# Running the 512-token feed-forward units as pairs of 64-row matmuls on two PSUM banks

## The chip, the cores and the metric

The kernel runs on one core of a Trainium2 chip. The metric is the device time of one execution in microseconds (us). The engines are named as in the profile: PE (TensorE matmul), PEld (its weight loads), DVE (VectorE), ACT (ScalarE), POOL (GpSimd), SP (SyncE, which only issues DMAs and waits).

## The reference

A gated linear-attention recurrence feeds two gated feed-forward layers; only the layers matter here (1536 tokens, width 320, hidden width 1536).

```python
def reference(**kwargs):
    attn_out = _attn_ref(**attn_kwargs)
    x = attn_out.transpose(0, 2, 1, 3).reshape(B * S, H * D)          # 1536 x 320
    x = _moe_ref(x=x, **moe_kwargs)
    return _moe2_ref(x=x, **moe2_kwargs)

def _moe_ref(x, w_gate, w_val, w_out):
    gate = 1.0 / (1.0 + np.exp(-(x @ w_gate)))
    val = x @ w_val
    return (gate * val @ w_out).astype(np.float32)
# _moe2_ref: the same without the sigmoid
```

## The kernel before

The hidden width is cut into 12 chunks of 128, so the two layers have 24 weight chunks. The tokens are cut into blocks of 512. Precision comes from splitting: every operand is held as a rounded part ("hi") and a remainder ("lo") in fp32r, and a product is hi·hi + lo·hi + hi·lo.

The work is a list of *units*: one chunk for one block of tokens. Units 0 to 23 have 256 tokens and run among the steps of the recurrence; units 24 to 83, 60 of them, have 512 tokens and fill the rest of the program. Four units that follow each other share one block and add into the same four accumulators; such a run of four is a *segment* (segment 8 is units 24 to 27, the last is segment 22). Each unit `u` is made of named tasks, and each task is a few instructions of one engine:

- `ma`, `mb` (PE): the gate and the value product, `mm1`, eight matmuls of 512 columns each into the banks `pa` and `pb`. The contraction of 320 is two full blocks of 128 rows, three matmuls each (hi·hi, hi·lo, lo·hi), and a block `c` of 64 rows, in which the weights' hi rows and lo rows lie in the two halves of the 128 rows, so that two matmuls do it.
- `ga_` (ACT, L549): the sigmoid (a copy in layer 2) of `pa`. `gm` (DVE, L554): times `pb`. `gh_` (ACT, L560) and `gl_` (DVE, L565): hi and lo of the result.
- `mm` (PE): 12 matmuls of 320 columns into the four accumulators `acc0` to `acc3`, three each.
- `ev` (DVE, L639, or L637 and ACT L635 in a layer's first segments): the four accumulators of a segment are added into `x2tok`.
- `yt`, `yh`, `yl`: after layer 1 each of 12 token tiles is transposed on PE (L483, three matmuls), and split on ACT (L492) and DVE (L496).

Each weight chunk is prepared by tasks of its own: `w` (a DMA of 960 KB, issued by SP), `na` (ACT, L214 and L215), `nb` (DVE, L221), `ns` (DVE, L226), `nc` (DVE, L232), `nd` (L238, on DVE or POOL), `s1` (ACT, L248 to L250), `s2` (L254, DVE or POOL) and `s3` (L258 and L259, DVE or POOL). Two buffers hold the staged weights, so `w` of a chunk waits until `s2` and `s3` of the chunk two before are done.

The order of everything is written out by hand in the string `PLAN`: each engine executes its instructions in the order in which the tasks stand there, and `:V` or `:G` says whether a task runs on DVE or POOL. PSUM is eight banks in four pairs of slots (`acc`, `mm1`, `e`, `y`), and a task that takes a slot waits until the last reader of that slot's former tile is done. `pa` comes from `mm1`, `pb` and the transposes from `e`.

`ga_` waits for `ma` alone, `gm` for `ga_` and `mb`, `mm` for `gl_` of its unit, and `ma` of unit u until `ga_` of unit u-2 has read its `pa`. What such a task looks like:

```python
        task("mm" + n, "P", lambda u=u: unit_mm2(u), ["gl_" + n] + prev("mm"), use)
```

Of the kernel before, what the change touches and what calls it, by code (L numbers as in the profile page):

```python
# [95 lines left out]
ev8.0 ga_30 s39:V ma31 w11 gm29 gh_29 gl_29 ma32 ev8.3 ga_31 na10 mb30 mb31 gm30 nb10 ev8.2 ma33 ns10 nc10
mm28 nd10:G mm29 gh_30 na11 gl_30 gm31 mm30 gh_31 ga_32 gl_31 mb32 s110 mm31 s210:G mb33 s310:G ev9.5 ev9.7
gm32 w12 ev9.4 gh_32 ma34 ga_33 gm33 gl_32 mb34 ev9.6 ga_34 nb11 gh_33 ns11 ma35 nc11 nd11:V mm32 s111 ma36
s211:V s311:G mb35 gl_33 ga_35 w13 mm33 gm35 gh_35 na12 gl_35 ma37 gm34 gh_34 mb36 gl_34 ga_36 mb37 ga_37 gm36
mm34 gm37 ma38 mm35 ma39 gh_36 ev10.11 gh_37 gl_36 ev10.9 ga_38 mb39 ev10.8 gl_37 ev10.10 ga_39 nb12 mb38 ns12  # L100
# [5 lines left out]
nc15 ma48 ev12.5 nd15:V gm47 s115 yt4 ma49 ev12.7 yh4 s215:G mm44 s315:G mm45 gh_46 gl_46 yl4 mb49 gh_47 ga_48
gl_47 ga_49 mm46 gm49 mm47 gh_49 gl_49 s214:V yt7 mb48 yh7 w16 yl7 w17 yt5 ma50 gm48 ev13.10 gh_48 ev13.8
gl_48 ma51 ev13.11 ev13.9 na16 mm48 yt6 yh5 mm49 ga_50 yl5 yh6 nb16 ga_51 ns16 mb50 yl6 yt9 ma52 gm50 yh9
gh_50 yl9 gl_50 yt10 mb51 yh10 mm50 gm51 nc16 gh_51 ga_52 ma53 gl_51 nd16:G yl10 mm51 mb52 ev14.2:A ev14.1:V
na17 ma54 ga_53 nb17 ev14.3:A ns17 s116 mb53 gm52 gh_52 s316:G gl_52 yt8 ma55 ev14.0:V yh8 gm53 ga_54 yl8  # L110
# [5 lines left out]
gm61 gh_61 mb63 ga_62 gl_61 ev16.9:V ga_63 mb62 s120 na21 ma64 s220:G gm62 gm63 mm60 s320:G w22 mm61 gh_63
gl_63 nb21 ma65 gh_62 ns21 gl_62 ga_64 mb64 ga_65 mm62 gm64 mm63 mb65 gh_64 ev17.0 nc21 ma66 nd21:V gm65 na22
ev17.3 mb66 ev17.1 ev17.2 gl_64 nb22 ga_66 ma67 gh_65 ns22 nc22 mb67 gl_65 ga_67 mm64 gm67 ma68 gh_67 s121
gl_67 nd22:V mm65 gm66 s221:V ma69 gh_66 s321:V gl_66 w23 ga_68 mb69 ga_69 mm66 gm69 mm67 ma70 mb68 ma71 gm68
ev18.7 gh_68 gl_68 mb70 ga_70 na23 mb71 gm70 ev18.4 s122 ev18.5 ev18.6 ma72 nb23 gh_69 ns23 s222:G mm68 nc23  # L120
# [823 lines left out]
```

## Time and profile before

| | us |
|---|---|
| median of 2 runs (453.55 and 454.4) | 453.98 |
| the profiled execution | 453.83 |
| its span, first to last instruction | 452.0 |
| start of unit 24's first matmul | 133.46 |

All durations are read from the one profiled execution, whose own time is 1.83 us above its span and 0.15 us under the median. The granted TensorE clock is 1.00, the level of 2.4 GHz, in every stretch until the very end. A matmul's record is longer than the step from one matmul to the next, because matmuls are pipelined: what counts on PE is the step.

### The profile page before, as it was taken

What the parts mean: (1) busy time and instruction counts of PE and PEld (TensorE: products, weight loads), DVE (VectorE), ACT (ScalarE), POOL (GpSimd) and SP (SyncE); (2) the same over time, 40 slices, a digit from 0 to 9 for tenths busy, and PEclk for the clock granted to TensorE, in tenths of its full rate; (3) what the DMA queues carried; (4) which work ended last, traced back from release to release, by engine and by line L of the source; (5) the groups of instructions that cost most, each with busy time, mean ns of one, the idle gap of its engine ahead of it and who ended that gap; (6) DMA issues with size and microseconds to landing.
All of it is one profiled execution on the core that took longest, in us unless ns stands there. A gap on an engine that the chain in (4) does not pass through costs nothing.

```text
span 452.0 us, 8740 instructions
## 1 busy us (share of the span) xinstructions
PE 441.0 (98%) x3530; PEld 394.8 (87%) x3530; DVE 298.7 (66%) x495; ACT 260.0 (58%) x455; POOL 121.6 (27%) x125
## 2 busy tenths in 40 slices
PE   8899999999999999999999999999999999999995
PEld 3577999899998989999999999897989898999995
DVE  6989999898853475747676666477574746534243
ACT  6989998787767556351656453756364425422220
POOL 3556573455143222210401320214222002300000
PEclk9999999999999999999999999999999999999998
DMA  7988534803201040220012040023122020000222
GB/s 237 261 277 286 157 113 143 293 2 119 88 0 56 33 146 30 89 87 1 9 80 87 1 175 1 0 88 96 80 88 88 0 88 1 0 1 5 55 58 59
DMA packets 10456, 39.33 MB, mean 87 GB/s; under 512 B 1840, under 2 KB 3760, under 8 KB 10416
## 3 DMA queue, kind: packets, MB, share of 16 engines
q1 hardware_dynamic: 10128, 38.45, 26.1%
q8 instruction: 28, 0.46, 0.4%
q10 hardware_dynamic: 288, 0.33, 0.2%
q14 instruction: 12, 0.10, 0.1%
HBM read 36.71 MB, written 1.97 MB: 86 GB/s over the span
## 4 chain that ended last, share of the span: by engine, by line
PE 82%; ACT 7%; DMA 4%; SPq 2%; issue 1%; DVE 1%; POOL 1%; POOLq 0%; ACTq 0%
PE pa L524 29%; PE pb L524 21%; PE acc L531 8%; PE acc L533 8%; PE acc L532 8%; PE o L441 2%; PE sp L412 2%; DMA og<-in_ogate_dram 2%; ACT cva L214 1%; DMA wst<-in_w_dram 1%; SPq L360 1%; PE st L431 1%; DMA cs<-in_cst_dram 1%; PE first L170 1%; ACT wst L215 1%
## 5 line engine op out<-in xcount | busy, mean ns | idle before, releaser
L524 PE MATMUL pa<-xb,W 128*128 128x512 f32 (+1 forms) x864 | 161.7, 335 | 1.1 <-ACT g L549 1.1
L524 PEld LDWEIGHTS pa<-xb,W 128*128 128x128 f32 x864 | 134.9, 190 | 13.8 <-ACT g L549 1.9
L524 PE MATMUL pb<-xb,W 128*128 128x512 f32 x480 | 112.6, 380 | 0.6 <-DVE g L554 0.6
L524 PEld LDWEIGHTS pb<-xb,W 128*128 128x128 f32 x480 | 89.3, 189 | 12.5 <-DVE g L554 1.0
L560 ACT ACTIVATE gh<-g 128x512 fp32r<-128x512 f32 (+1 forms) x84 | 47.5, 568 | 87.7 <-DVE g L554 44.2
L531 PE MATMUL acc<-W,gh 128*128 128x320 f32 x288 | 87.0, 302 | 0.0
L533 PE MATMUL acc<-W,gl 128*128 128x320 f32 x288 | 86.4, 300 | 0.0
L532 PE MATMUL acc<-W,gh 128*128 128x320 f32 x288 | 86.1, 299 | 0.0
L565 DVE TENSOR_TENSOR gl<-g,gh 128x512 fp32r<-128x512 f32 (+1 forms) x67 | 48.8, 735 | 44.3 <-ACT gh L560 44.0
L554 DVE TENSOR_TENSOR g<-g,pb 128x512 f32<-128x512 f32 x60 | 40.8, 685 | 55.4 <-PE pb L524 43.3
L549 ACT ACTIVATE g<-pa 128x512 f32<-128x512 f32 x60 | 35.7, 598 | 37.2 <-DVE gl L565 32.8
L531 PEld LDWEIGHTS acc<-W,gh 128*128 128x128 f32 x288 | 54.5, 189 | 1.4
L532 PEld LDWEIGHTS acc<-W,gh 128*128 128x128 f32 x288 | 54.5, 189 | 1.3
L533 PEld LDWEIGHTS acc<-W,gl 128*128 128x128 f32 x288 | 54.4, 189 | 0.4 <-DVE gl L565 0.3
L238 POOL TENSOR_TENSOR wst<-cva,wst 128x960 int32<-128x960 int32 x10 | 23.6, 2357 | 77.2 <-DVE cva L232 51.5
L214 ACT ACTIVATE cva<-wst 128x960 f32<-128x960 f32 x24 | 32.1, 1338 | 16.5 <-DVE wst L238 9.6
L254 POOL TENSOR_TENSOR W<-wst,W 128x832 fp32r<-128x832 f32 x9 | 19.2, 2137 | 71.2 <-ACT W L248 62.7
L248 ACT ACTIVATE W<-wst 128x832 fp32r<-128x832 f32 x24 | 28.6, 1191 | 13.6 <-DVE wst L238 9.9
L639 DVE SCALAR_TENSOR_TENSOR x2tok<-acc,x2tok 128x320 f32<-128x320 f32 x52 | 23.5, 484 | 15.0 <-PE acc L533 14.9
L215 ACT ACTIVATE wst<-wst 128x960 int32<-128x960 uint32 x24 | 31.1, 1295 | 0.0
L232 DVE SCALAR_TENSOR_TENSOR cva<-wst,cva 128x960 int32<-128x960 int32 x24 | 30.2, 1259 | 0.4
L565 POOL TENSOR_TENSOR gl<-g,gh 128x256 fp32r<-128x256 f32 x17 | 13.9, 818 | 35.7 <-ACT gh L560 25.8
(88 smaller groups left out, 494.2 us busy)
## 6 DMA issues: line engine op xcount, KB each, us to landing
wst<-in_w_dram SPq DMA_DIRECT2D x24, 960.0 KB
kq<-in_kqT_dram SPq DMA_DIRECT2D x12, 512.0 KB
Y<-in_kv_dram SPq DMA_DIRECT2D x24, 162.0 KB
out_dram<-x2tok SPq DMA_DIRECT2D x10, 160.0 KB
og<-in_ogate_dram SPq DMA_DIRECT2D x1, 960.0 KB
og<-in_ogate_dram SPq DMA_DIRECT2D x1, 640.0 KB
cs<-in_cst_dram SPq DMA_DIRECT2D x1, 469.0 KB
rhsE<-V SPq DMA_DIRECT2D x24, 2.0 KB
```

Of the source, the lines that this page charges most:

```text
L214: nc.scalar.activation(cva[0], hi.bitcast(F32), AF.Abs)
L215: nc.scalar.activation(lo, lo.bitcast(U32), AF.Copy, scale=2.0**-29)
L232: nc.vector.scalar_tensor_tensor(ai, hi, -0x40000000, ai, op0=ALU.bitwise_and, op1=ALU.bitwise_or)
L248: nc.scalar.activation(w[:, 0:NH], g[:, 0:NH], AF.Copy)
L524: nc.tensor.matmul(dst, w[:, w0 : w0 + P], x[:, h, cb].rearrange("p a b -> p b a"), start=(i == 0), stop=(i == 7))
L531: nc.tensor.matmul(a, gh[:, c], wh, start=st, stop=False)
L532: nc.tensor.matmul(a, gh[:, c], wl, start=False, stop=False)
L533: nc.tensor.matmul(a, gl[:, c], wh, start=False, stop=sp)
L549: nc.scalar.activation(t, pa, AF.Copy if l else AF.Sigmoid)
L554: nc.vector.tensor_tensor(t, t, pb, op=ALU.mult)
L560: nc.scalar.activation(gh, g, AF.Copy)
L565: eng.tensor_tensor(gl, g, gh.bitcast(F32), op=ALU.subtract)
```

## The change

In the 60 units of 512 tokens every matmul of 128 rows becomes a matmul of 64 rows, and two of them are issued as a pair: one on rows 0 to 63 of the array (LOW), one on rows 64 to 127 (UPP), on different PSUM banks. A unit's gate and value products are no longer one after the other: `ma` runs LOW rows into `pa` beside UPP rows into `pb` (8 pairs), `mb` the other way round (7 pairs). The 64-row block needs only hi·hi, hi·lo and lo·hi, so 30 half matmuls do what 16 full ones did: 15 pairs. The second product is split in the same way, `mm` with 6 pairs and a new task `mn` with 6, 12 pairs for 12 matmuls.

Where the halves exchange banks (from `ma` to `mb`, from `mm` to `mn`) the first pair must not start before the last pair has left its banks. It waits for an instruction on SP that does nothing but wait for the last two matmuls. `ga_` now waits for `mb`, as `pa` is complete only then. `pa` and `pb` are taken together at `ma`. The transposes of layer 1's output move from the slots `e` to `mm1`. `PLAN` is rewritten from unit 24 on into a regular pattern, one line of it before and after:

```diff
-gh_25 ma27 mb26 gl_25 mm24 nc8 k111:V gm26 ga_27 nd8:G mm25 w9 mb27 na9 ma28 gh_26 gl_26 ma29 gm27 gh_27 ga_28
+mb29 na10 mn27 ma30 ga_29 ev8.1 ev8.0 ev8.3 ev8.2 gm29 mm28 gh_29 gl_29 nb10 ns10 mb30 nc10 nd10:V mn28 w11
...
+    def side_by_side(runs, after=()):
+        turn = None
+        if after:
+            turn = nc.sync.nop()
+            for m in after:
+                tc.add_manual_dep(turn.ins, m.ins.name, sync)
+        for pair in zip(*runs):
+            last = [nc.tensor.matmul(o, w, x, start=st, stop=sp) for o, w, x, st, sp in pair]
+            if turn is not None:
+                for m in last:
+                    tc.add_manual_dep(m.ins, turn.ins.name, sync)
+                turn = None
+        return last
+
+    def tiles(rows, m):
+        a, al, c = m * 2 * P, NH + m * 2 * P, 2 * NH + m * P
+        own = [(c, 0, 2), (c, 1, 2)] if (rows is LOW) == (m == 0) else [(c, 0, 2)]
+        return [y for i in range(2) for y in ((a + i * P, 0, i), (a + i * P, 1, i), (al + i * P, 0, i))] + own
+
+    def mm1_half(f, l, x, dst, part, after):
+        w = W[l * NF + f]
+        runs = []
+        for rows, m in ((LOW, part), (UPP, 1 - part)):
+            t = tiles(rows, m)
+            runs.append([
+                (dst[m], w[rows, w0 : w0 + P], x[rows, h, cb].rearrange("p a b -> p b a"), part == 0 and i == 0, part == 1 and i == len(t) - 1)
+                for i, (w0, h, cb) in enumerate(t)
+            ])
+        return side_by_side(runs, after)
+
+    def mm2_half(f, l, gh, gl, accs, part, swap, st, sp, after):
+        w = W[l * NF + f]
+        wh, wl = (w[:, k + 4 * P : k + NH].rearrange("p (a b) -> p b a", a=2) for k in (0, NH))
+        runs = []
+        for rows, j0 in ((LOW, 2 * (part ^ swap)), (UPP, 2 - 2 * (part ^ swap))):
+            runs.append([
+                (accs[j], g[rows, j * P : (j + 1) * P], o[rows], st and part == 0 and k == 0, sp and part == 1 and k == 2)
+                for j in (j0, j0 + 1)
+                for k, (g, o) in enumerate(((gh, wh), (gh, wl), (gl, wh)))
+            ])
+        return side_by_side(runs, after)
...
     def ph_T2(s):
-        Tps[NSTEP + s] = transp(ps_tile("e", f"t2_{s}"), x2tok[:, s])
+        Tps[NSTEP + s] = transp(ps_tile("mm1", f"t2_{s}"), x2tok[:, s])
...
-        task("ga_" + n, "A", lambda u=u: unit_act(u), [("mb" if small else "ma") + n] + prev("ga_"), [("g", ["gl_" + n])] + ([("ge", ["gm" + n])] if pre else []))
+        task("ga_" + n, "A", lambda u=u: unit_act(u), ["mb" + n] + prev("ga_"), [("g", ["gl_" + n])] + ([("ge", ["gm" + n])] if pre else []))
...
+        if not small:
+            task("mn" + n, "P", lambda u=u: unit_mm2b(u), ["mm" + n])
```

The changed kernel's line numbers are shifted: L549 is every paired matmul, L603 is `gm`, L614 is `gl_`, L704 is `ev`, L485 the transposes, L533 to L535 the second product of the units of 256 tokens.

Three places show the new order. On PE, the first transposes of layer 1's output (`t2_0`) stand before the change between the second product of unit 41 and the first product of unit 43, all of them matmuls of the whole array:

```order
781 L532 MATMUL acc12_3_3088<-W9_2472,gh41_3031 128x320
782 L533 MATMUL acc12_3_3088<-W9_2472,gl41_3046 128x320
783 L483 MATMUL t2_0_3116<-cs_87,x2tok_88 128x128 x3
784 L524 MATMUL pb43_3120<-xb1_1155,W11_2729 128x512 x8
785 L524 MATMUL pa45_3140<-xb2_1729,W9_2472 128x512 x8
```

After the change they stand between `ma44` and `mm42`, and what stands around them are pairs of 64 rows:

```order
1569 L549 MATMUL pa44_3659<-xb2_1729,W8_2346 128x512
1570 L549 MATMUL pb44_3660<-xb2_1729,W8_2346 128x512
1573 L485 MATMUL t2_0_3680<-cs_87,x2tok_88 128x128 x3
1574 L549 MATMUL acc12_0_3536<-W10_2770,gh42_3623 128x320
1575 L549 MATMUL acc12_2_3538<-W10_2770,gh42_3623 128x320
```

There are 12 such groups, each between pairs now.

On DVE, around the evacuation of segment 9 (`acc9`; `g` and `gl` with a number are those of a unit, `cva11` and `wst11` belong to the preparation of chunk 11), the four additions stand before the change ahead of that preparation and among `gm` and `gl`:

```order
262 L554 TENSOR_TENSOR g31_2535<-g31_2535,pb31_2549 128x512
263 L565 TENSOR_TENSOR gl31_2625<-g31_2535,gh31_2621 128x512
264 L639 SCALAR_TENSOR_TENSOR x2tok_88<-acc9_1_2573,x2tok_88 128x320
265 L639 SCALAR_TENSOR_TENSOR x2tok_88<-acc9_3_2575,x2tok_88 128x320
266 L554 TENSOR_TENSOR g32_2623<-g32_2623,pb32_2627 128x512
267 L639 SCALAR_TENSOR_TENSOR x2tok_88<-acc9_0_2572,x2tok_88 128x320
270 L639 SCALAR_TENSOR_TENSOR x2tok_88<-acc9_2_2574,x2tok_88 128x320
271 L221 TENSOR_SCALAR cva11_2603<-cva11_2603 128x960
```

After the change they stand behind `gl32` and the four DVE steps of chunk 11:

```order
267 L603 TENSOR_TENSOR g32_2876<-g32_2876,pb32_2788 128x512
268 L614 TENSOR_TENSOR gl32_2893<-g32_2876,gh32_2891 128x512
269 L223 TENSOR_SCALAR cva11_2842<-cva11_2842 128x960
270 L228 TENSOR_SCALAR cva11_2842<-cva11_2842 128x960
271 L234 SCALAR_TENSOR_TENSOR cva11_2842<-wst11_2716,cva11_2842 128x960
272 L240 ISA wst11_2716<-wst11_2716,cva11_2842 128x960x2
273 L704 SCALAR_TENSOR_TENSOR x2tok_88<-acc9_1_2665,x2tok_88 128x320
274 L704 SCALAR_TENSOR_TENSOR x2tok_88<-acc9_3_2667,x2tok_88 128x320
```

The preparation of a chunk has moved ahead of an evacuation that PE needs for its next segment.

On PE, where the 512-token units begin (`acc7` is the second product of the last 256-token units), `pb25` follows `pa25` directly before the change:

```order
614 L524 MATMUL pa25_2275<-xb0_534,W5_1598 128x512 x7
615 L524 MATMUL pb25_2286<-xb0_534,W5_1598 128x512 [waits PE_49]
616 L524 MATMUL pb25_2286<-xb0_534,W5_1598 128x512 x7
617 L531 MATMUL acc7_0_2203<-W2_877,gh22_2231 128x320 [waits Activation_49]
```

After the change the two last small products stand inside unit 25, and the next pair waits for SP, where the load `w9` is ahead of its wait in `PLAN`:

```order
653 L549 MATMUL pa25_2291<-xb0_534,W5_1598 128x512
654 L549 MATMUL pb25_2292<-xb0_534,W5_1598 128x512
655 L533 MATMUL acc7_0_2203<-W2_877,gh22_2231 128x320 [waits Activation_49]
666 L535 MATMUL acc7_1_2204<-W3_940,gl23_2268 128x320 [waits Pool_49]
667 L549 MATMUL pb25_2292<-xb0_534,W5_1598 128x512 [waits SP_sequencer_49]
```

The matmul that exchanges banks has got a wait on SP, and one more change between whole-array and 64-row matmuls on either side.

## Rows read from the trace of the kernel before

**Rows 1.** The page, busy time of engines: us, share of the span, instructions.

```profile
PE 441.0 (98%) x3530; PEld 394.8 (87%) x3530; DVE 298.7 (66%) x495; ACT 260.0 (58%) x455; POOL 121.6 (27%) x125
```

**Rows 2.** Waits of PE from 133 to 447 us: total, times, longest.

```profile
PE pa L524 <- ACT g L549: 1.1, 1, 1.1
PE pb L524 <- DVE g L554: 0.6, 1, 0.6
```

**Rows 3.** Timeline of PE, full array: start us, length us, matmuls.

```profile
132.24 0.30 PE L531 MATMUL acc<-W,gh 128*128 128x320 f32 x1
132.38 0.30 PE L532 MATMUL acc<-W,gh 128*128 128x320 f32 x1
...
133.46 1.89 PE L524 MATMUL pa<-xb,W 128*128 128x512 f32 x8
135.19 1.89 PE L524 MATMUL pb<-xb,W 128*128 128x512 f32 x8
```

**Rows 4.** Timelines of PE and PEld near 60.8 us: 64-row matmuls of the recurrence.

```profile
60.78 0.65 PE L397 MATMUL sp<-kq,cs 40*64 40x512 f32 x2
60.80 0.68 PE L412 MATMUL sp<-kq 40*64 40x64 f32 x16
...
60.78 0.14 PEld L397 LDWEIGHTS sp<-kq,cs 40*64 40x64 f32 x2
60.79 0.14 PEld L412 LDWEIGHTS sp<-kq 40*64 40x64 f32 x2
```

**Rows 5.** Timeline of PE where it changes from 64-row to 128-row matmuls.

```profile
88.97 0.22 PE L412 MATMUL sp<-kq 40*64 40x64 f32 x2
89.13 0.40 PE L531 MATMUL acc<-W,gh 128*128 128x320 f32 x1
```

**Rows 6.** Groups of DVE by shape: busy us, mean ns; idle before, releaser.

```profile
L565 DVE TENSOR_TENSOR gl<-g,gh 128x512 fp32r<-128x512 f32 x60 | 45.4, 763 | 44.2 <-ACT gh L560 44.0
L554 DVE TENSOR_TENSOR g<-g,pb 128x512 f32<-128x512 f32 x60 | 40.8, 685 | 55.4 <-PE pb L524 43.3 <-ACT g L549 12.0
L232 DVE SCALAR_TENSOR_TENSOR cva<-wst,cva 128x960 int32<-128x960 int32 x24 | 30.2, 1259 | 0.4
L639 DVE SCALAR_TENSOR_TENSOR x2tok<-acc,x2tok 128x320 f32<-128x320 f32 x52 | 23.5, 484 | 15.0 <-PE acc L533 14.9
L238 DVE CUSTOM_DVE_ANT_0 wst<-wst,cva 128x1920 uint16<-128x1920 uint16 x14 | 19.1, 1363 | 0.4
L221 DVE TENSOR_SCALAR cva<-cva 128x960 f32<-128x960 f32 x24 | 15.9, 663 | 6.1 <-ACT cva L214 5.9
L226 DVE TENSOR_SCALAR cva<-cva 128x960 int32<-128x960 int32 x24 | 15.9, 661 | 0.5
```

**Rows 7.** Groups of ACT by shape, same columns.

```profile
L560 ACT ACTIVATE gh<-g 128x512 fp32r<-128x512 f32 x60 | 37.7, 631 | 81.2 <-DVE g L554 44.2 <-PE acc L532 36.8
L549 ACT ACTIVATE g<-pa 128x512 f32<-128x512 f32 x60 | 35.7, 598 | 37.2 <-DVE gl L565 32.8 <-PE pa L524 3.5 <-PE pb L524 0.8
L214 ACT ACTIVATE cva<-wst 128x960 f32<-128x960 f32 x24 | 32.1, 1338 | 16.5 <-DVE wst L238 9.6 <-POOL wst L238 4.7 <-DMA wst<-in_w_dram 2.1
L215 ACT ACTIVATE wst<-wst 128x960 int32<-128x960 uint32 x24 | 31.1, 1295 | 0.0
L248 ACT ACTIVATE W<-wst 128x832 fp32r<-128x832 f32 x24 | 28.6, 1191 | 13.6 <-DVE wst L238 9.9 <-POOL wst L238 3.6
...
L250 ACT ACTIVATE W<-wst 64x128 fp32r<-64x128 f32 x24 | 8.1, 336 | 0.5
```

**Rows 8.** Groups of POOL by shape, same columns.

```profile
L254 POOL TENSOR_TENSOR W<-wst,W 128x832 fp32r<-128x832 f32 x9 | 19.2, 2137 | 71.2 <-ACT W L248 62.7 <-issue 8.5
L565 POOL TENSOR_TENSOR gl<-g,gh 128x256 fp32r<-128x256 f32 x17 | 13.9, 818 | 35.7 <-ACT gh L560 25.8 <-DVE xt L473 6.2 <-PE acc L533 1.9
L258 POOL TENSOR_TENSOR W<-wst,W 64x128 fp32r<-64x128 f32 x16 | 11.9, 747 | 34.0 <-ACT W L249 25.5 <-issue 7.8
```

**Rows 9.** SP's waits: line and what it waited for, total us, times, longest.

```profile
SPq L207 <- DVE W L254: 137.0, 12, 29.7
```

More of the change, by code (lines that the diff above doesn't have):

```diff
@@ L96 @@
[L96 to L100, printed above, removed]
@@ L106 @@
[L106 to L110, printed above, removed]
@@ L116 @@
[L116 to L120, printed above, removed]
@@ L126 @@
-gh_81 ma83 gl_81 ga_82 ev21.5 out5 mb82 ga_83 mm80 gm82 mb83 gh_82 mm81 gm83 gl_82 mm82 gh_83 gl_83 mm83
-ev22.8 ev22.9 out9 ev22.10 ev22.11 out11
+mm20 gh_21 ga_22 gp22 gl_21:G gm22 nd7:G ga_23 na8 gh_22 gp23 k011:G gl_22:G mm21 s17 gm23 ma24 gh_23 gl_23:G
+nb8 ns8 s37:G mb24 nc8 nd8:V ma25 ga_24 gm24 mm22 mm23 gh_24 gl_24 s27:G w9 mb25 s18 ma26 ga_25 gm25 gh_25
+gl_25 s28:G s38:V ev7.11:V ev7.10:A mm24 mb26 na9 mn24 ma27 ga_26 gm26 mm25 gh_26 gl_26 nb9 ns9 k111:V mb27
+nc9 nd9:V mn25 w10 ma28 ga_27 gm27 mm26 gh_27 gl_27 mb28 s19 mn26 ma29 ga_28 gm28 mm27 gh_28 gl_28 s29:G s39:V
@@ new lines @@
+mb29 na10 mn27 ma30 ga_29 ev8.1 ev8.0 ev8.3 ev8.2 gm29 mm28 gh_29 gl_29 nb10 ns10 mb30 nc10 nd10:V mn28 w11
+ma31 ga_30 gm30 mm29 gh_30 gl_30 mb31 s110 mn29 ma32 ga_31 gm31 mm30 gh_31 gl_31 s210:G s310:V mb32 na11 mn30
+ma33 ga_32 gm32 mm31 gh_32 gl_32 nb11 ns11 mb33 nc11 nd11:V mn31 w12 ma34 ga_33 ev9.5 ev9.7 ev9.4 ev9.6 gm33
+mm32 gh_33 gl_33 mb34 s111 mn32 ma35 ga_34 gm34 mm33 gh_34 gl_34 s211:G s311:V mb35 na12 mn33 ma36 ga_35 gm35
+mm34 gh_35 gl_35 nb12 ns12 mb36 nc12 nd12:V mn34 w13 ma37 ga_36 gm36 mm35 gh_36 gl_36 mb37 s112 mn35 ma38
@@ new lines @@
+mb45 nc15 nd15:V mn43 w16 ma46 ga_45 ev12.4 ev12.6 ev12.5 ev12.7 gm45 yt2 mm44 yh2 yl2 gh_45 gl_45 mb46 s115
+mn44 ma47 ga_46 gm46 yt3 mm45 yh3 yl3 gh_46 gl_46 s215:G s315:V mb47 na16 mn45 ma48 ga_47 gm47 yt4 mm46 yh4
+yl4 gh_47 gl_47 nb16 ns16 mb48 nc16 nd16:V mn46 w17 ma49 ga_48 gm48 yt6 mm47 yh6 yl6 gh_48 gl_48 mb49 s116
+mn47 ma50 ga_49 ev13.10 ev13.8 ev13.11 ev13.9 gm49 yt5 mm48 yh5 yl5 gh_49 gl_49 s216:G s316:V mb50 na17 mn48
+ma51 ga_50 gm50 yt7 mm49 yh7 yl7 gh_50 gl_50 nb17 ns17 mb51 nc17 nd17:V mn49 w18 ma52 ga_51 gm51 yt10 mm50
@@ L128 @@
+mb77 mn75 ma78 ga_77 ev20.2 ev20.3 ev20.0 ev20.1 gm77 mm76 gh_77 gl_77 mb78 mn76 ma79 ga_78 gm78 mm77 gh_78
+gl_78 mb79 mn77 out1 out3 ma80 ga_79 gm79 mm78 gh_79 gl_79 mb80 mn78 ma81 ga_80 gm80 mm79 gh_80 gl_80 mb81
+mn79 ma82 ga_81 ev21.6 ev21.7 ev21.4 ev21.5 gm81 mm80 gh_81 gl_81 mb82 mn80 out7 ma83 ga_82 gm82 mm81 gh_82
+gl_82 mb83 mn81 out5 ga_83 gm83 mm82 gh_83 gl_83 mn82 mm83 mn83 ev22.8 ev22.9 out9 ev22.10 ev22.11 out11
 """
@@ L624, in unit_mm2, with mm2_part, unit_mm2b @@
         UT[u]["accs"] = dict(accs)
+        if ns == 4:
+            UT[u]["mm"] = mm2_part(u, 0, ())
+            return
         mm2(f, l, UT[u]["gh"], UT[u]["gl"], [accs[i] for i in range(ns)], f == fs[0], f == fs[-1])
+    def mm2_part(u, part, after):
+        k, f = UNITS[u]
+        l, fs, t = SEGS[k][0], SEGS[k][3], UT[u]
+        return mm2_half(f, l, t["gh"], t["gl"], t["accs"], part, fs.index(f) % 2, f == fs[0], f == fs[-1], after)
+    def unit_mm2b(u):
+        mm2_part(u, 1, UT[u]["mm"])
     def unit_evac(u, i, e):
@@ L751 @@
         task("xl" + n, "V", lambda s=s: ph_xl(s), ["xh" + n])
+    ends = lambda u: "mm" if SEGS[UNITS[u][0]][2] == 2 else "mn"
     staged = {k: [f"sg{i}" for i in range(len(OGS)) if OGS[i][2] == k] for k in {o[2] for o in OGS}}
@@ L797 @@
                 before = [f"yt{s}"]
-            task(f"ev{k}.{s}", on, (lambda e, u=u, i=i: unit_evac(u, i, e)) if len(on) > 1 else (lambda u=u, i=i: unit_evac(u, i, nc.vector)), ["mm" + n] + before)
+            task(f"ev{k}.{s}", on, (lambda e, u=u, i=i: unit_evac(u, i, e)) if len(on) > 1 else (lambda u=u, i=i: unit_evac(u, i, nc.vector)), [end + n] + before)
             if last and l and s % 2:
```

63 lines of the change are left out of this document (36 added, 27 removed).

## Prediction, made before the changed kernel ran

> **What bounds the kernel now.** I read the page first: PE is busy for 441.0 of 452.0 us, DVE for 66% and ACT for 58% [rows 1]. So the next view is who makes PE wait. From unit 24 on (133 to 447 us) PE waited twice, 1.1 and 0.6 us, both times for a gate that came late [rows 2]. The rest of those 314 us is matmul after matmul, so the stretch is worth what its steps add up to. The timeline gives the steps: eight matmuls of 512 columns take from 133.46 to 135.19 us, 0.216 each; two of 320 columns stand 0.136 apart (132.24 and 132.38, both rounded) [rows 3]. A unit is 16 × 0.216 + 12 × 0.136 = 5.09 us, and 60 units are 305 us. Loading weights costs nothing extra there: PEld is busy for 394.8 us under the 441.0 of PE [rows 1].
>
> **The change, part by part.** All is counted against the profiled execution, 453.83 us, which is 0.15 under the median.
>
> *The pairs.* What matters is whether a pair takes the step of one matmul. No pair of 64 rows by 128 columns is in the trace, but the recurrence has 64-row matmuls on different rows and banks. At 60.78 us two of 512 columns begin together (one piece, x2, 0.65 us long), and while they run sixteen of 64 columns go by on the other quarters of the array; four weight loads of 0.14 us lie within 0.15 us [rows 4]. Loads and products of different rows do run side by side. So I take 0.216 and 0.136 per pair. A unit has 15 + 12 pairs instead of 16 + 12 matmuls, and saves one step: 60 × 0.216 = **-13.0**. The bound on the bad side is that the two loads of a pair follow each other: a rival below. A bound on the good side: no step can be shorter than its columns, so -13.0 is all of it.
>
> The Trainium skill (TensorE: Matmul & The Clock Gate, "Measured speedup vs the span model") gives about 4 ns of issue per further tile; by it the sum would be 60 × 27 × 0.004 = 6.5 us higher, an estimate from that page. In rows 4 the second of two 512-column matmuls begins so close to the first that the timeline prints one start for both, and a late start need not add up where each half has its own rows; I leave it out of the sum.
>
> *Waits that go.* In the new order `nd` is on DVE throughout and each chunk is ready more than a unit before its use, so the two late gates should go: **-1.7** [rows 2].
>
> *Transposes among pairs.* Now 12 groups of whole-array transposes stand between 64-row pairs: 24 changes of tile size. Rows 5 show one: the last two 64-column matmuls start at 88.97, the first whole-array one at 89.13, 0.16 later where 0.06 is usual (sixteen in 0.68 minus one record of 0.22 [rows 4, 5]), and its record is 0.40 instead of 0.30, since its load lies bare. That is 0.20 per change, and I take the same the other way round: 24 × 0.20 = **+4.8**. Bounds: nothing, if a wait hides it, and twice that, if the two loads of a pair both lie bare.
>
> *Exchanges through SP.* There are 120. The last matmul of eight ends 0.16 after its last step (1.89 long, 1.73 between starts [rows 3]); a bare load is 0.10 [rows 5]; the passage through SP has no row, and I add 0.1 (at least nothing; at most some tenths): 0.4 us, where nothing covers it. Between `ma` and `mb` stand the six pairs of an earlier `mm` (0.82 us), between `mm` and `mn` an `mb` (1.51). So 117 cost nothing, and if that cover failed each would cost up to 0.4. Bare are `mb24`, `mn82` and `mn83`: **+1.2**. What is queued behind such a wait on SP are weight loads, which are early by several units, and in the other direction the wait can stand behind a weight load:
>
> *The beginning.* `w9` stands on SP ahead of the wait of `mb25`, and needs `s2` of chunk 7, on POOL. From the start of `ma24` ACT has `na8` (1.34 + 1.30) and `s1` of chunk 7 (1.19 + 2 × 0.34), then POOL the rest of unit 23 (0.82), `s3` (two, 0.75 each) and `s2` (2.14) [rows 7, 8]: 9.0 us. PE reaches `mb25` after 1.73 + 0.4 + 1.51 + 1.73 + 2 × 0.82 and two changes of tile size (0.4): 7.4. It waits about 1.5. Then `mm24` needs the last evacuation of segment 7, which stands on DVE behind `gl` of unit 25 and `s3` of chunk 8: from the end of `mb25` 0.16 + 0.60 + 0.69 + 0.63 + 0.76 + 0.48 = 3.3 without that `s3`, 4.8 with it at POOL's rate [rows 6 to 8]; PE has only `ma26`, 1.73. It is 1.6 to 3.1 late; I take 1.9, near the low end, as DVE's steps are the shorter ones. With three changes of tile size (0.6) the beginning costs **+4.0**; between 1.0 (nobody late) and 7.
>
> *Evacuations behind a weight chunk.* The pattern prepares a chunk every three units and evacuates every four, so once in 12 units DVE has `nb` to `nd` directly ahead of the evacuation. For segment 9: ACT has from `gh` of unit 30 to `ga` of unit 32 `s1` (1.86), `ga` and `gh` of unit 31 with `gm` between (0.60 + 0.69 + 0.63) and `na11` (2.63), 6.4 us, while PE goes from the end of `mb31` to that of `mb32` in 4.9; taking `gh` of unit 30 as done when `mb31` ends, gate 32 starts 1.5 late. From there 0.60 + 0.69 + 0.63 + 0.76, then `nb` to `nd` 0.66 + 0.66 + 1.26 + 1.36, then three evacuations of 0.48, since `mm32` begins on the accumulators that come free first and third: 8.1 [rows 6, 7]. DVE is there 9.6 us after `mb32`, PE already after 7.4 (`mn30`, `ma33`, `mm31`, `mb33`, `mn31`, `ma34`). Late by 2.1, of which a little is regained: 2.0. The same holds for the segments 12 and 18; at 15 ACT takes one of the four, and I count 0.5: **+6.5**. Bounds: nothing and 9. Otherwise DVE keeps up: in three units it has 3 × (0.69 + 0.63 waiting + 0.76) + 3.9 + 1.5 for `s3` + 1.5 = 13.1 us, PE 14.6.
>
> Sum: -13.0 - 1.7 + 4.8 + 1.2 + 4.0 + 6.5 = **+1.8, 455.6 us**. A measurement tells about 2% from no change, that is under 444.9 or over 463.1.
>
> **Rivals.**
>
> *DVE is not late.* If the evacuations and the beginning cost only the changes of tile size, it is 453.83 - 14.7 + 4.8 + 1.2 + 0.6 = 445.7, and some us less if a change of tile size is partly hidden. For it: DVE was idle 34% of the span [rows 1], and gates ready in advance would absorb 2 us. Against: the order leaves these chains no room by the count above.
>
> *SP as a queue.* The pivot is the wait for a weight load that is not ready: before the change SP spent 137 us in `w` waiting for `s2` alone [rows 9]. If each of the 14 loads after `w9` holds up a matmul as `w9` does, 1.5 us, the time is 455.6 + 21 = 476.6; it decides as soon as `s2` of the chunk two before ends later than the next wait. Against it: `w10` on stand one to two units behind the `s2` and `s3` that they need.
>
> *The two loads of a pair follow each other.* Then a pair cannot be shorter than two loads, 2 × 0.11 or so (a bare load is 0.10 [rows 5]): 27 × 0.22 = 5.9 instead of 4.87 per unit, +64 in all: 520. Rows 4 speak against it.
>
> *Weights cannot be loaded under a matmul of the same rows.* Each pair would show a load of 0.10: 60 × 27 × 0.10 = +162, 618 us. The Trainium skill says so (TensorE: Matmul & The Clock Gate, "The mechanism", under "What overlaps and what doesn't": only where the row group differs). The trace does not agree with it for whole-array matmuls: they share all rows, and PEld is busy 87% under a PE busy 98% [rows 1].
>
> *A pair is no pair.* If the halves run one after the other, a unit costs 30 × 0.216 + 24 × 0.136 = 9.7: +279, 735 us. Against: rows 4.
>
> **How the numbers follow.** The forecast has 0.60, its own range 450 to 461 (the bounds of the last two parts, not all at once). DVE not late 0.23, half of it under 444.9. SP as a queue 0.08, loads in turn 0.05, bare loads 0.02, no pairs 0.02. Faster by over 2%: 0.12. Slower: the upper edge of the forecast, 0.03, and the last four, 0.17: 0.20. Within 2%: 0.68. The range leaves out the lowest part of the second case and what lies above 470: 444 to 470.
>
> **What would show it right or wrong.** Right: pairs of 512 columns 0.216 apart and of 320 columns 0.136; PE idle about 2 us before `mm32`, `mm44` and `mm68`, put down to DVE; 1.5 us before `mb25`, put down to SP; 0.2 on either side of each transpose group; no idle time at the other exchanges. Wrong: pair steps above 0.22 and 0.14, idle PE at every `mb`, or no idle PE at the evacuations.

## The result, and the profile after

The changed kernel takes 459.37 us (459.29 and 459.45) against 453.98: a ratio of 1.0119, 95% interval 1.0075 to 1.0162. It is slower by 5.4 us, which is under 2%, but the interval does not reach 1; the forecast was 455.6, 1.6 us slower. The profiled execution took 459.29 us with a span of 457.5, 5.5 above the span before.

The page, the same row as in [rows 1]: PE is busy for 5.7 us less (435.3 against 441.0) in a span that is 5.5 longer:

```profile
PE 435.3 (95%) x5085; PEld 401.8 (88%) x5090; DVE 300.7 (66%) x512; ACT 258.0 (56%) x455; POOL 107.7 (24%) x108
```

So matmuls were saved and waits were added. The waits of PE from 133 to 452 us (engine and line waited for, total, times, longest) stand against the two of [rows 2]:

```profile
PE acc L549 <- DVE x2tok L704: 3.6, 3, 1.5
PE pb L549 <- SPq L545: 2.7, 1, 2.7
PE acc L549 <- DVE x2tok L702: 2.6, 2, 2.2
PE acc L535 <- POOL gl L614: 0.4, 1, 0.4
```

L704 and L702 are evacuations (`ev`), L545 is the exchange of `mb25` through SP. The gates of [rows 2] are gone from the list. Of 120 exchanges only one stands in it (a bare one leaves PE idle for 0.1 us, too little for the list).

Next, do pairs keep the step? The timeline of PE in `ma24` and at its exchange (start, length, tile, times):

```profile
134.36 0.38 PE L549 MATMUL pa<-xb,W 64*128 64x512 f32 x1
134.36 0.38 PE L549 MATMUL pb<-xb,W 64*128 64x512 f32 x1
134.58 0.38 PE L549 MATMUL pa<-xb,W 64*128 64x512 f32 x1
134.58 0.38 PE L549 MATMUL pb<-xb,W 64*128 64x512 f32 x1
...
135.23 0.95 PE L549 MATMUL pb<-xb,W 64*128 64x512 f32 x2
135.70 0.48 PE L549 MATMUL pa<-xb,W 64*128 64x512 f32 x1
136.02 0.38 PE L549 MATMUL pb<-xb,W 64*128 64x512 f32 x1
```

Both halves begin together (in the trace's records the second starts 3 to 4 ns behind the first), a pair every 0.216 us, as one matmul did in [rows 3]. `mb24` is an exchange with nothing to cover it: the step before it is 0.475 instead of 0.216, and the one behind it 0.32, since its load lies bare: 0.36 in all. At the 116 exchanges other than `mb24`, `mb25`, `mn82` and `mn83` the step is the usual one to 0.001 us.

A group of transposes between pairs, on PE:

```profile
241.48 0.38 PE L549 MATMUL pb<-xb,W 64*128 64x512 f32 x1
241.78 0.55 PE L485 MATMUL t<-cs,x2tok 128*128 128x128 f32 x3
242.26 0.54 PE L549 MATMUL acc<-W,gh 64*128 64x320 f32 x4
```

The step into the group (241.48 to 241.78) is 0.30 instead of 0.22, the group takes 0.48 (three steps of 0.11 would be 0.33), and the four matmuls behind it, two pairs, last 0.10 longer than elsewhere (0.54 against 0.43): 0.34 to 0.35 for the two changes of tile size, twelve times.

Now the beginning. The timeline of all engines from `ma25` to `mb25`:

```profile
137.49 1.74 POOL L614 TENSOR_TENSOR gl<-g,gh 128x256 fp32r<-128x256 f32 x1 [3.58 <-PE pa L549]
...
139.77 1.06 POOL L614 TENSOR_TENSOR gl<-g,gh 128x256 fp32r<-128x256 f32 x1 [0.54 <-ACT gh L609]
...
140.91 0.46 POOL L260 TENSOR_TENSOR W<-wst,W 64x128 fp32r<-64x128 f32 x1
...
141.40 0.30 PE L535 MATMUL acc<-W,gl 128*128 128x320 f32 x1
...
141.96 4.38 POOL L256 TENSOR_TENSOR W<-wst,W 128x832 fp32r<-128x832 f32 x2
...
143.98 0.33 SPq L209 DMA_DIRECT2D wst<-in_w_dram  x1
...
144.42 0.79 PE L549 MATMUL pb<-xb,W 64*128 64x512 f32 x1 [2.72 <-SPq L545]
144.42 0.79 PE L549 MATMUL pa<-xb,W 64*128 64x512 f32 x1
145.00 0.63 PE L549 MATMUL pb<-xb,W 64*128 64x512 f32 x1
...
145.43 0.63 PE L549 MATMUL pb<-xb,W 64*128 64x512 f32 x1
```

PE is done with `mm23` at 141.7 and has nothing to wait for but SP. SP stands at `w9`, `w9` waits for `s2` of chunk 7 on POOL (the first of the two in the row at 141.96), and goes out at 143.98; `mb25` begins behind it. Then something that was in no step of the forecast: the pairs are 0.43 apart. The same stretches with the granted clock (window, busy, instructions, clock, DMA share, GB/s):

```profile
133.60:141.50 7.90, 7.41 (x59) 1.00 0.01 2
141.50:144.40 2.90, 0.20 (x2) 0.90 0.00 0
144.40:147.40 3.00, 2.98 (x14) 0.52 0.78 266
```

Behind a stretch in which PE stood still for 2.7 us the clock fell to the level of 1.2 GHz for about seven pairs, some 1.4 us more. After that PE waited 2.2 us at `mm24` for `ev7.11` (L702 in the list of waits).

Last, one of the evacuations behind a chunk, `mm32`, on DVE and PE:

```profile
186.94 0.69 DVE L614 TENSOR_TENSOR gl<-g,gh 128x512 fp32r<-128x512 f32 x1 [0.75 <-ACT gh L609]
187.54 0.65 DVE L223 TENSOR_SCALAR cva<-cva 128x960 f32<-128x960 f32 x1
...
190.50 1.18 DVE L240 CUSTOM_DVE_ANT_0 wst<-wst,cva 128x1920 uint16<-128x1920 uint16 x1
191.58 0.90 DVE L704 SCALAR_TENSOR_TENSOR x2tok<-acc,x2tok 128x320 f32<-128x320 f32 x2
192.22 0.37 PE L549 MATMUL acc<-W,gh 64*128 64x320 f32 x1 [1.47 <-DVE x2tok L704]
```

`gl` of unit 32 ends at 187.6, then DVE has 4 us of chunk 11, and only then the additions, for which `mn31`, whose last matmul ends at 189.0, had been ready.

To put the whole together I took, step by step from the first pair to the last, how far apart two starts are beyond the usual step (0.216, 0.136, 0.109), in both traces:

| term | predicted | measured |
|---|---|---|
| one step of 512 columns less in 60 units | -13.0 | -13.0 |
| waits that go | -1.7 | -2.9 |
| changes of tile size at 12 transpose groups | +4.8 | +4.2 |
| bare exchanges `mb24`, `mn82`, `mn83` | +1.2 | +1.2 (0.36, 0.49, 0.36) |
| the beginning, up to `mm24` | +4.0 | +7.8 |
| evacuations at `mm32`, `mm44`, `mm56`, `mm68` | +6.5 | +6.4 (2.3, 1.4, 0.8, 1.9) |
| ahead of `ma24` | 0 | +0.15 |
| behind the start of the last matmul | 0 | +1.2 |
| sum | +1.8 | +5.1 of the 5.5 between the spans |

The remaining 0.4 is spread over small steps. From `ma24` to the last matmul it is 317.5 us against 313.4.

### The profile page after: what moved, and what is told of

Its sections match the earlier page's. It is cut to its first block, busy times and chain, and to the rows that moved or that the text cites. A ratio compares the mean times of both kernels' runs of the same rounds, so it can differ in the third digit from the quotient of the medians.

```text
span 457.5 us, 12013 instructions
## 1 busy us (share of the span) xinstructions
PE 435.3 (95%) x5085; PEld 401.8 (88%) x5090; DVE 300.7 (66%) x512; ACT 258.0 (56%) x455; POOL 107.7 (24%) x108
## 4 chain that ended last, share of the span: by engine, by line
PE 76%; ACT 8%; DVE 8%; DMA 3%; issue 2%; POOL 1%; SPq 1%; DVEq 0%; ACTq 0%; POOLq 0%
PE acc L549 19%; PE pb L549 17%; PE pa L549 17%; PE pa L526 9%; PE o L443 2%; PE sp L414 2%; DMA wst<-in_w_dram 2%; DVE cva L234 2%; DMA og<-in_ogate_dram 1%; PE acc L533 1%; ACT gh L609 1%; PE acc L534 1%; PE acc L535 1%; PE st L433 1%; DVE wst L240 1%
## 5 line engine op out<-in xcount | busy, mean ns | idle before, releaser
L549 PE MATMUL pb<-xb,W 64*128 64x512 f32 x900 | 214.8, 378 | 2.8 <-SPq L545 2.7
L549 PE MATMUL pa<-xb,W 64*128 64x512 f32 x900 | 214.8, 378 | 0.0
L549 PEld LDWEIGHTS pb<-xb,W 64*128 64x128 f32 x900 | 162.4, 187 | 5.8 <-SPq L545 3.5
L549 PEld LDWEIGHTS pa<-xb,W 64*128 64x128 f32 x900 | 162.4, 187 | 2.9 <-issue 0.2
L549 PE MATMUL acc<-W,gh 64*128 64x320 f32 x960 | 114.5, 301 | 6.3 <-DVE x2tok L704 3.6
L549 PEld LDWEIGHTS acc<-W,gh 64*128 64x128 f32 x960 | 102.1, 186 | 12.3 <-issue 5.9
L549 PE MATMUL acc<-W,gl 64*128 64x320 f32 x480 | 90.5, 296 | 0.0
L603 DVE TENSOR_TENSOR g<-g,pb 128x512 f32<-128x512 f32 x60 | 41.1, 685 | 65.7 <-ACT g L598 65.7
L614 DVE TENSOR_TENSOR gl<-g,gh 128x512 fp32r<-128x512 f32 (+1 forms) x67 | 45.7, 682 | 37.5 <-ACT gh L609 37.0
L549 PEld LDWEIGHTS acc<-W,gl 64*128 64x128 f32 x480 | 65.5, 186 | 0.1
L526 PE MATMUL pa<-xb,W 128*128 128x256 f32 x384 | 48.4, 277 | 0.0
L526 PEld LDWEIGHTS pa<-xb,W 128*128 128x128 f32 x384 | 46.0, 192 | 0.7
L704 DVE SCALAR_TENSOR_TENSOR x2tok<-acc,x2tok 128x320 f32<-128x320 f32 x52 | 22.2, 487 | 14.0 <-PE acc L549 13.9
L614 POOL TENSOR_TENSOR gl<-g,gh 128x256 fp32r<-128x256 f32 x17 | 15.2, 895 | 32.5 <-ACT gh L609 13.3
```

The source lines that it names most:

```text
L526: nc.tensor.matmul(dst, w[:, w0 : w0 + P], x[:, h, cb].rearrange("p a b -> p b a"), start=(i == 0), stop=(i == 7))
L549: last = [nc.tensor.matmul(o, w, x, start=st, stop=sp) for o, w, x, st, sp in pair]
L603: nc.vector.tensor_tensor(t, t, pb, op=ALU.mult)
L614: eng.tensor_tensor(gl, g, gh.bitcast(F32), op=ALU.subtract)
```

## The experiments

In these sets the median of the kernel before was 453.1 to 454.3 us, single executions lay between 450.9 and 459.2, and in the profiles the part ahead of `ma24`, which no experiment touches, took 131.6 to 137.5 us. So beside each ratio I read the *tail*, from the start of `ma24` to that of the last matmul: 313.4 before, 317.5 after the change. A tail is that of one execution each. What speaks for reading it to tenths is that stretches which a run leaves alone repeat: from `ma44` to `ma56` it took 68.23 us after the change and in runs 1, 5, 8 and 10. In the lines of the experiments the pairs are L546, `ev` L699, L701 and, on ACT, L697, unless said otherwise.

**1. `w9` behind the exchange of `mb25`.**

```diff
-s27:G w9 mb25 s18 ma26
+s27:G mb25 w9 s18 ma26
```

> Only the place of w9 on SP changes: it stands behind the exchange wait of mb25 instead of ahead of it. In the changed kernel mb25 waited 2.9 us and its first seven pairs then ran at half the clock (0.427 apart instead of 0.216), some 1.4 us more. My theory (the weight load on SP held the matmul): mb25 starts about 0.15 after the last matmul of mm23, the clock stays at 1.00, and what is left waits at mm24: s1 of chunk 8 and then gate 25 on ACT (144.4 + 0.6), gm, gh, gl, s3 of chunk 8 and ev7.11 put it near 148.2 us instead of 151.5. So about 3.3 us less, 456.0. Rival (the chain from gate 24 over POOL and DVE sets mm24 anyway): mb25 goes early, mm24 still begins near 151.5, and the time stays within 0.5 of 459.3.

Measured: 458.1 us, ratio 1.0086 (1.0045 to 1.0128), tail 318.0. The exchange is out of the waits, and the evacuation has taken its place (4.0 for L699, 3.7 of it before `mm24`; after the change 2.6 and 2.2):

```profile
PE acc L546 <- DVE x2tok L699: 4.0, 2, 3.7
PE acc L546 <- DVE x2tok L701: 3.7, 3, 1.5
PE acc L532 <- POOL gl L611: 0.4, 1, 0.4
```

`mm24` begins 15.2 us after `ma24` instead of 17.9: 2.7 of the 3.3 that I expected there. But nothing is left of it in the tail. The clock fell behind this longer wait, and once more behind the wait at `mm32` (1.5 us idle), where it had not fallen in the changed kernel:

```profile
147.40:150.40 3.00, 3.00 (x18) 0.50 0.00 0
...
189.50:193.70 4.20, 4.15 (x27) 0.73 0.02 4
```

So my theory was right on SP and wrong on the time: two things stand in a row at the beginning, SP's queue and `ev7.11`, and taking the first alone hands the wait to the second. My theory had counted on a clock that stays at 1.00.

**2. `nc` and `nd` behind the evacuations.** Chunk 11 here; 15, 19 and 23 alike.

```diff
-nb11 ns11 mb33 nc11 nd11:V mn31 w12 ma34 ga_33 ev9.5 ev9.7 ev9.4 ev9.6 gm33 mm32 gh_33 gl_33 mb34
+nb11 ns11 mb33 mn31 w12 ma34 ga_33 ev9.5 ev9.7 ev9.4 ev9.6 gm33 mm32 nc11 gh_33 gl_33 nd11:V mb34
```

> Four places of PLAN: nc and nd of chunks 11, 15, 19 and 23 stand behind the evacuation of segments 9, 12, 15 and 18 instead of ahead of it. My theory: PE's waits before mm32, mm44, mm56 and mm68 (2.4, 1.6, 0.8 and 1.6 us beyond the steps, 6.4 in all) go, since DVE reaches the first addition when mn31, mn43, mn55 and mn67 end; gates 33, 45, 57 and 69 are no later than they were. About 6.2 us less, 453.1. Rival (DVE has no spare time in these stretches): the wait comes back at mm33, mm45, mm57 and mm69, or at the next chunk, and less than 2 us are gained.

Measured: 455.12 us, ratio 1.0014 (0.9973 to 1.0054), tail 312.9, 4.6 less, of which 1.0 came before `ma28`, where nothing was changed (the half clock lay elsewhere). So 3.5 of 6.4. The four waits are gone, and new ones have come:

```profile
PE acc L546 <- ACT x2tok L697: 1.0, 1, 1.0
PE acc L546 <- DVE x2tok L699: 0.9, 1, 0.9
PE t L482 <- ACT g L595: 0.7, 1, 0.7
...
PE acc L546 <- DVE x2tok L701: 0.3, 1, 0.3
```

The 0.9 is `mm24`'s, there before; the others are new, before `mm60`, a transpose and `mm36`. The timeline of ACT shows how one of them comes:

```profile
252.90 1.31 ACT L247 ACTIVATE W<-wst 128x832 fp32r<-128x832 f32 x1 [2.14 <-DVE wst L237]
...
254.84 0.60 ACT L595 ACTIVATE g<-pa 128x512 f32<-128x512 f32 x1
```

L247 is `s1` of chunk 15. ACT stood 2.1 us for the `nd` that had been moved, and gate 46 stood behind it. The wait had left DVE and gone over to ACT.

**3. The saved pair given back.** Of the change only 15 against 16 pairs is undone.

```diff
-        own = [(c, 0, 2), (c, 1, 2)] if (rows is LOW) == (m == 0) else [(c, 0, 2)]
+        own = [(c, 0, 2), (c, 1, 2)]
```

> The only thing undone is the saved pair: mb has 8 pairs instead of 7, as the 64-row block is given a fourth product (remainder by remainder), so a unit has 16 + 12 steps as before the change. My theory (PE's steps set the time, and the saving is worth 0.216 a unit): 60 x 0.216 = 13.0 us more, less what the four late evacuations and the beginning regain with a longer mb (some 5 x 0.2 = 1), about 12.0 more: 471.3. Rival (a unit is set by the chain of gates on ACT and DVE, and PE waits for it anyway): under 6 us more.

Measured: 470.75 us, ratio 1.0341 (1.0272 to 1.0411), tail 326.8, 9.3 more. 60 steps are 13.0; 2.1 were regained at the evacuations, as a longer unit leaves DVE more time, and 1.6 at the beginning, where the clock stayed at 1.00 in this execution. Where nothing waits, from `ma76` to `mm83`, it took 42.79 against 41.06: 1.73 for eight units, 0.216 each. The rival (under 6) is out: the steps of PE are what a unit costs.

**4. Transposes in groups of two.**

```diff
-ma44 ga_43 gm43 yt0 mm42 yh0 yl0 ... ma45 ga_44 gm44 yt1 mm43 yh1 yl1
+ma44 ga_43 gm43 yt0 yt1 mm42 yh0 yl0 yh1 yl1 ... ma45 ga_44 gm44 mm43
```

> The 12 groups of transposes become 6 groups of two, the second of each in a slot of e, so 12 changes of tile size instead of 24. In the changed kernel a group cost 0.35 beyond its steps (0.09 before it, 0.05 within, 0.09 and 0.10 behind it). My theory (the change between whole-array and 64-row matmuls is what costs): 6 x 0.35 = 2.1 us less, 457.2, if ACT and DVE split the second transpose in time for the next ma. Rival (each transpose costs what it costs, or the pair of transposes waits for its splits): within 0.5 of 459.3, with six groups that cost 0.7 each or a wait of ma for yl.

Measured: 459.87 us, ratio 1.0122 (1.0058 to 1.0185), tail 318.9. From `ma44` to `ma56`, where the groups are, it took 68.0 us against 68.2: nothing gained. The waits name the reason:

```profile
PE t L482 <- DVE g L600: 3.0, 2, 2.3
```

The second transpose of a group takes a slot of `e`, which is free only when `gm` of the unit before has read it, and two groups stood behind a `gm` that DVE did late. That is the second half of the rival. Its first half is out: where a group of two did not wait (before `mm46`, `mm48` and `mm52`), it cost 0.35 beyond its steps, as much as one transpose did; the waits took the gain away.

**5. Another beginning.**

```diff
-mb24 nc8 nd8:V ma25 ga_24 gm24 mm22 mm23 gh_24 gl_24 s27:G w9 mb25 s18 ma26 ga_25 gm25 gh_25
-gl_25 s28:G s38:V ev7.11:V ev7.10:A mm24 mb26 na9 mn24 ma27 ga_26 gm26 mm25 gh_26
+ma25 mb24 nc8 nd8:V ga_24 mm22 mm23 ev7.10:A gm24 ev7.11:V gh_24 gl_24 s27:G mb25 w9 ma26 ga_25 gm25 gh_25
+gl_25 s18 s28:G s38:V mm24 mb26 mn24 ma27 ga_26 gm26 mm25 gh_26 na9
```

> Only the beginning of the 512-token units is put in another order: ma25 between ma24 and mb24, both evacuations of segment 7 right behind mm23 and ahead of gl of unit 24, w9 behind the exchange wait of mb25, s1 of chunk 8 behind gate 25, na9 behind gate 26. In the run with w9 alone moved, mm24 began 15.2 us after ma24 and waited 3.8 us for ev7.11. My theory (mm24 is late only because ev7.11 stands behind gate 25 and s3 of chunk 8): mm24 begins as soon as PE reaches it, 9.64 + 1.73 = 11.4 us after ma24 at the latest, against 17.9 in the changed kernel; no pair runs at half the clock there. About 6.6 us less, 452.7. Rival (the table load, gate 24 and gl of unit 24 on ACT, DVE and POOL are the chain): gl of unit 24 ends 11 us after ma24 in that run, and if it moves later with the additions put ahead of it, mm24 begins at 13 or later and less than 5 us are gained.

Measured: `mm24` begins 11.4 us after `ma24`, to the tenth as PE reaches it, and the clock stays up (window, busy, clock as above):

```profile
137.00:157.00 20.00, 19.43 (x186) 1.00 0.20 60
```

`ma28` is reached 6.6 us earlier than in the changed kernel. The tail is 311.8, 5.7 less, since 0.9 is given back at `mm28` and `mm32`, whose evacuations PE now reaches earlier. 455.71 us, ratio 1.0043 (1.0008 to 1.0077); in this profile the part ahead of `ma24` took 137.5. The rival (13 or later) is out: `ev7.11` was late by the order. Which of the moved tasks was needed for it this run does not tell apart.

**6. Evacuations first, and `s1` later.** As 2, and for the same four chunks:

```diff
-mb34 s111 mn32 ma35 ga_34
+mb34 mn32 ma35 ga_34 s111
```

> As the earlier run that moved nc and nd behind the evacuations, and s1 of these chunks behind ga of the unit after next as well. In that run two new waits came (0.9 us for a gate before a transpose group, 1.2 us before mm60), each some units after an s1 that stands on ACT and waits for the nd that was moved. My theory (ACT stood still at s1, and the gates behind it came late): the new waits go, all of the 6.4 us of the four evacuations are kept, 453.0 and a tail from ma24 to the last matmul 6 us shorter than the changed kernel's 317.5. Rival (DVE itself has no time for the chunk and the evacuation in one unit): the new waits stay or move, and the tail is shorter by no more than 4.5 us.

Measured: 452.9 us, ratio 0.9961 (0.9919 to 1.0004), tail 310.3, 7.2 less than the changed kernel, 0.4 of it before `ma28`. All that is left in PE's waits belongs to the beginning:

```profile
PE pb L546 <- SPq L542: 2.7, 1, 2.7
PE acc L546 <- DVE x2tok L699: 1.5, 1, 1.5
PE acc L532 <- POOL gl L611: 0.4, 1, 0.4
```

DVE had the time. What it lacked was the order, and with DVE's order ACT's had to be moved too.

**7. The same, with transposes in groups of two at other units.**

```diff
-... gm43 yt0 mm42 ... gm44 yt1 mm43 ... gm45 yt2 mm44 ... gm46 yt3 mm45
+... gm43 yt0 yt1 mm42 ... gm44 yt2 yt3 mm43 ... gm45 mm44 ... gm46 mm45
```

> The run with evacuations first and s1 late, with six groups of two transposes, put at units whose predecessor's gm is done early (before mm42, mm43, mm46, mm48, mm49, mm52). In the earlier run with groups of two, two groups waited 3.0 us for gm, since the slot of e is free only then. My theory (a change of tile size costs what it costs, whatever stands between): no such wait, and 6 x 0.35 = 2.1 us less than the run without groups of two. Rival (the cost belongs to each transpose): no difference beyond 0.3 us.

Measured: 448.87 us, ratio 0.9875 (0.9812 to 0.9937), tail 307.7. From `ma44` to `ma56` 64.6 us against 66.5 of run 6: 2.0 less, where 2.1 was expected, and no wait of a transpose in the list. The cost lies in the change between whole-array and 64-row matmuls, not in the transposes.

**8. Twenty bare exchanges.** In ten units:

```diff
-ma72 ... mm70 ... mb72 ... mn70
+ma72 mb72 ... mm70 mn70
```

> In ten units (mb72 to mb81, mn70 to mn79) the order ma mm mb mn becomes ma mb mm mn, so that 20 more exchanges have nothing between the halves. My theory (the wait through SP costs about 0.36 us where it is bare, 0.26 before the pair and 0.10 behind its bare load, as at mb24, mn82 and mn83): 20 x 0.36 = 7.2 us more than the changed kernel, all of it between ma72 and mn81; so the cover of 117 exchanges is worth about 42 us. Rival (SP's passage is hidden in part by the pipeline, or queues up): under 4 us more, or over 11.

Measured: 467.68 us, ratio 1.0283 (1.0217 to 1.035), tail 323.5. From `mm68` to `mm80` 66.1 us against 58.7: 7.4 for 20. Each looks like `mb24`; here `mb72`:

```profile
386.92 0.95 PE L546 MATMUL pb<-xb,W 64*128 64x512 f32 x2
387.39 0.48 PE L546 MATMUL pa<-xb,W 64*128 64x512 f32 x1
387.71 0.38 PE L546 MATMUL pb<-xb,W 64*128 64x512 f32 x1
```

0.47 and 0.32 instead of 0.216 twice. So an exchange costs 0.36 to 0.37 bare and nothing behind six pairs, and the interleaving of `ma`, `mm`, `mb`, `mn` is worth some 117 × 0.37 = 43 us, an estimate from these 20. The beginning of this run is that of the changed kernel, with the same 2.7 us for SP, and yet:

```profile
142.30:146.00 3.70, 3.50 (x30) 1.00 0.78 264
```

The clock did not fall, and from `mb25` to `mm24` it took 5.7 us instead of 7.1: 1.4 is what the half clock cost.

**9. All together**: 5, 6, 7 and 10.

> All that was shown to help, together: the other beginning, evacuations ahead of nc and nd with s1 later, transposes in six groups of two, and the second product of units 82 and 83 in whole-array matmuls again (accumulator after accumulator, no exchange at the end). From ma24 to the last matmul the run with the evacuations and groups of two took 307.7 us and reached ma28 25.0 after ma24; with the other beginning that was 19.4. My theory (the losses are separate and add up): 307.7 - 5.6 - 0.5 at the last units = 301.6, and 0.8 less behind the last matmul, as three of four accumulators are complete before it. Against the 318.5 of the kernel before from ma24 to the end some 307: 11.7 us less than before, 441.5. Rival (with PE 12 us ahead, the chunks or the gates become late and take back what was gained): tail of 305 or more, 445 or more.

Measured: 442.69 us, ratio 0.9756 (0.9708 to 0.9805): faster than the kernel before, and than the changed one. Tail 302.4 (301.6 expected). The page and the two waits that are left from 132 us on (`ev` is L703 here):

```profile
PE 429.7 (98%) x5061; PEld 389.1 (88%) x5066; DVE 303.6 (69%) x512; ACT 258.7 (59%) x455; POOL 105.8 (24%) x108
```

```profile
PE acc L532 <- POOL gl L611: 0.5, 1, 0.5
PE acc L546 <- DVE x2tok L703: 0.2, 1, 0.2
```

PE is busy 98% again, as in [rows 1], for 429.7 us instead of 441.0. The rival (445 or more) is out.

**10. The last two units in whole-array matmuls.**

```diff
-mn81 out5 ga_83 gm83 mm82 gh_83 gl_83 mn82 mm83 mn83 ev22.8
+mn81 out5 ga_83 gm83 mm82 gh_83 gl_83 mm83 ev22.8
...
+    WHOLE = {82, 83}
...
-        if ns == 4:
+        if ns == 4 and u not in WHOLE:
             UT[u]["mm"] = mm2_part(u, 0, ())
```

> Only the second product of units 82 and 83 is put back to whole-array matmuls, 12 each, accumulator after accumulator. In the changed kernel the exchanges mn82 and mn83 cost 0.36 each, and the time from the last matmul's start to the end was 6.38 us against 5.16 before, as all four additions begin when the last accumulators are nearly done. My theory: 0.7 - 0.2 (one change of tile size) less before the last matmul, and 0.8 less behind it (four additions of 0.48 begin while matmuls still run): 1.3 us less, 458.1. Rival (the time behind the last matmul is set by the stores): 0.5 less, and 6.2 or more behind the last matmul as in the changed kernel.

Measured: tail 317.2; 0.43 less from `mm24` on, and behind the last matmul's start 5.50 instead of 6.38, 0.88 less: 1.3 together, as expected. The time, 459.19 us (ratio 1.0123, 1.0045 to 1.0202), does not show it. Where the 0.9 lies is in the timeline of the end, first of the changed kernel:

```profile
451.02 1.30 DVE L704 SCALAR_TENSOR_TENSOR x2tok<-acc,x2tok 128x320 f32<-128x320 f32 x3 [1.67 <-PE acc L549]
451.10 0.30 PE L549 MATMUL acc<-W,gl 64*128 64x320 f32 x2
```

and of run 9, where the last units are whole:

```profile
433.94 1.71 DVE L703 SCALAR_TENSOR_TENSOR x2tok<-acc,x2tok 128x320 f32<-128x320 f32 x4 [0.49 <-PE acc L532]
...
434.82 0.30 PE L532 MATMUL acc<-W,gl 128*128 128x320 f32 x1
```

Pairs add into two accumulators at a time, so all four become ready near the end, and the four additions begin 0.1 us ahead of the last matmul. Accumulator after accumulator they begin 0.9 ahead of it.

## Why the prediction came out as it did

*Pairs: right.* The step is 0.216 and 0.136 [rows 3 and the timeline of `ma24`], and run 3 prices it: giving the pair back costs what it says, less what the late evacuations and the clock at the beginning gave. The estimate after the Trainium skill (TensorE: Matmul & The Clock Gate, "Measured speedup vs the span model"), 4 ns for each further tile, would make a pair's step 0.220. The trace has such a delay, 3 to 4 ns from one half of a pair in `ma24` to the other, but it does not add up: the step stays at 0.216. (That two starts are printed as one in [rows 4] was no sign of it, as the timeline merges such rows; the records there are 7 ns apart.) The three rivals on loads and pairs fall with it. The price of the last one was worked out against the unit before the change and added to the forecast; it should have been 748 us and not 735, which changes no choice.

*Evacuations behind a weight chunk: right.* 6.4 against 6.5, by the chain that the prediction counted, `gl`, `nb` to `nd`, additions; gate 32 started 1.5 behind the end of `mb32`, as counted. The sum is nearer than its parts: 0.3 more at `mm32` and `mm56`, 0.6 less at `mm44`, 0.1 less at `mm68`. Runs 2 and 6 show that it is the order, and the rival that DVE is not late (445.7 us) is out.

*Tile sizes and exchanges: right.* 0.35 for a group instead of 0.40; 0.36 for an exchange, which is 0.16 + 0.10 and the guessed 0.1 for the passage before they were rounded to 0.4, and nothing where it is covered. `mn82` took 0.12 more, as the halves ahead of it ran 0.13 apart. Runs 7 and 8 show both alone.

*SP as a queue* was one wait, not fourteen: `w10` and those behind it held up nothing.

*The beginning is the step that failed in its size*: "between 1.0 (nobody late) and 7", 4.0 taken, 7.8 measured. In its parts: the three changes 0.6, as said. `w9` was 2.7 and not 1.5, because `s2` of chunk 7 ended 10.4 us after `ma24` and not 9.0: the two `gl` ahead of it on POOL took 1.74 and 1.06 where [rows 8] has 0.82 (both beside `nc` and `nd` of chunk 8 on DVE; whether that made them longer no run shows), and the second waited for its `gh`, which ACT does behind `s1`. The same late `gl` held `mm23` itself, 0.66, which I had not counted. `mm24` waited 2.5 and not 1.9. And the half clock, 1.4, was in no term.

*Left out altogether*: the end. The prediction followed PE to its last matmul and took what lies behind it as unchanged. It is 1.2 longer, 0.9 by the additions that all come last (run 10). The other 0.3 lies behind the issue of the last stores: from there to the end it is 4.0 us, and 3.9 in run 10, but 3.6 before the change and in runs 6, 7 and 9; the reason stays open. *Waits that go* were 2.9 and not 1.7: a wait also lays bare the load behind it (0.1), its step is longer than the idle time in the list by 0.1 to 0.2, and three steps 0.2 late are in no list of waits.

The three misses that cost time are 3.8, 1.2 and 0.15; tile sizes, the waits that went and the evacuations gave back 1.9.

The larger reading holds: the change saves 13 us on PE and spends them on places where another engine's order was fitted to the old pattern. None of these losses belongs to the pairs themselves, except the changes of tile size and the bare exchanges, 4.2 and 1.2, and 0.6 for the three changes at the beginning.

## What to carry to other kernels

When PE is busy 98% of the time, a change that shortens its steps is paid only where every other engine's in-order queue is early enough: list, for each engine, what stands ahead of the one instruction that PE waits for next, and reorder that together with the change. Moving one late task often hands the wait to the next one in the row (runs 1 and 4 gained nothing and run 2 half; runs 5, 6 and 7, which moved what stood behind it as well, gained nearly all of it). Price a change between whole-array and 64-row matmuls at about 0.17 us each way and a wait through SP at 0.36 us bare, and put independent matmuls between.
